# Two gate/up steps on raw x: normalising after the matmul instead of before it

## The chip, the cores and the metric

The kernel runs on one core of one Trainium2 chip. The metric is the device time of one execution in microseconds (us). A core has TensorE (PE in the profile, with its weight loads as PEld), VectorE (DVE), ScalarE (ACT), GpSimd (POOL) and SyncE (SP). SP does no arithmetic here; it issues DMA transfers, and so do ACT and GpSimd. Names such as "SPq" in a profile line mean the issuing queue of that engine.

## The reference, cut to what matters

```python
def reference(A_x, A_w_r, A_w_i, B_x, B_w_gate, B_w_up, B_w_down):
    x = A_x                                        # (1, 2048, 640) bf16
    xn = _layernorm(x, axis=-1)                    # (x - mean) / sqrt(var + 1e-5), per row
    s = irfft2(rfft2(xn) * (w_r + 1j * w_i))       # the spectral branch
    g = _silu((_gelu(xn @ w_gate) * (xn @ w_up)) @ w_down)   # 640 -> 1536 -> 640
    return x + s * g
```

Everything starts from the layer norm of x. The kernel treats the 2,048 rows as 16 slabs of 128 rows and as 4 groups of 512 rows. For each group there are 12 gate/up steps (128 of the 1,536 columns each), and then the down product. The spectral branch is a chain of "folds" (additions on VectorE), Fourier matrices on TensorE, a regrouping through DRAM and the inverse; it fills TensorE between the steps.

## The kernel before

A static planner in the program orders all work on every engine; each piece is added with a rank, an estimated duration and the pieces it comes after. The parts that the change and the argument touch are these.

The start: loads of x and of the first weights, and warm-up matmuls on zeros, which keep TensorE busy until the first slab is ready.

```python
    nc.scalar.dma_start(out=X[64:P, 0, :], in_=xv[64:P, 0, :])
    nc.scalar.dma_start(out=X[:, 2, :], in_=xv[:, 2, :])
    ...
    x_in[0] = dma(X[0:64, 0, :], xv[0:64, 0, :], (0, -4, seq[0]), 163840, use=[sX])
    load_x(1, 2)
    load_x(3, 4)
    ...
    t = keep_warm(8, [t])
    warmed = keep_warm(1, [t, x_in[1]], ns=216)
    load_gu(0, 2)          # Wg and Wu, columns 0 to 255
    load_x(4, 6)
    load_gu(2, 4)
    ...
```

The normalisation of one slab: statistics, the root on GpSimd, the application on VectorE, the transposition on TensorE, and its copy out of PSUM.

```python
            nc.vector.bn_stats(out=STAT[:, n1, 6 * g:6 * g + 6], in_=x[:, 320 * g:320 * g + 320])     # DVE slabs
            nc.scalar.activation(out=junk.tile, in_=x, func=ACT.Square, scale=1.0, bias=NM[:, n1, :], accum_out=var)  # ACT slabs
            ...
            nc.gpsimd.tensor_tensor(out=rstd, in0=var, in1=mh, op=ALU.pow)                            # 1/sigma
            ...
            nc.vector.tensor_scalar(out=sxn.tile[:, n1 % 2, :], in0=X[:, n1, :], scalar1=..., scalar2=RSTD[:, n1, :],
                                    op0=ALU.subtract if eng == "DVE" else ALU.add, op1=ALU.mult)
            ...
                nc.tensor.transpose(out=pt.tile[:, c, :], in_=sxn.tile[:, n1 % 2, c * P:c * P + P], identity=ident)
        turned[n1] = add(lambda e: copy_on(e, xnT[:, :, n1 * P:(n1 + 1) * P], pt.tile), ...)
```

One gate/up step. The first two steps of group 0 are computed slab by slab (128 columns of the result at a time), so that they can begin with the first slab.

```python
            parts = [(128 * j, 128 * j + 128) for j in range(4)] if grp == 0 and t < 2 else [(0, 512)]
            ...
                        nc.tensor.matmul(ps.tile[:, lo:hi], lhsT=w[:, c, t * P:(t + 1) * P],
                                         rhs=xnT[:, c, grp * 512 + lo:grp * 512 + hi], start=(c == 0), stop=(c == 4), ...)
            ...
            nc.scalar.activation(out=ge.tile, in_=pg.tile, func=ACT.Gelu_apprx_tanh)
            nc.vector.tensor_tensor(out=u.tile, in0=pu.tile, in1=ge.tile, op=ALU.mult)
```

Of the kernel before, what the change touches and what calls it, by code (L numbers as in the profile page):

```python
# [11 lines left out]
FP32 = mybir.dt.float32  # L12
# [3 lines left out]
P = 128  # L16
# [98 lines left out]
class Plan:  # L115
# [12 lines left out]
    def add(self, emit, eng, cost, rank, after=(), new=(), use=(), size=0, slow=1.0, hold=0, order=(), lag=0):  # L128
        engs = eng if isinstance(eng, dict) else {eng: cost}
        t = Task(emit=emit, engs=engs, rank=rank, after=list(after), new=list(new), size=size, slow=slow, hold=hold, order=list(order), lag=lag,  # L130
                 seq=len(self.tasks))
        for s in (*new, *use):
            s.users.append(t)
        self.tasks.append(t)
        return t

    def ready(self, t, e, now):
        for a in t.after:
            if a.done is None:
                return None  # L140
        for a in t.order:
            if a.start is None:
                return None
        at = max([0.0] + [a.start + a.engs[e][0] if a.on == e == "PE" else a.done + (0 if a.on == e and not a.size else self.MARGIN[e] + ((2500 if a.size else 250) if e == "PE" and a.start > 20000 else 0)) for a in t.after])
        more = {}
        for s in t.new:
            mine = self.slots[s.tag]
            k = len(mine) - self.bufs[s.tag] + more.get(s.tag, 0)
            more[s.tag] = more.get(s.tag, 0) + 1
            if k >= 0:  # L150
                for u in mine[k].users:
                    if u.done is None:
                        return None
                    at = max(at, u.done + self.MARGIN[e])
        if t.size and e == "SP":
            at = max(at, self.wire - self.BACKLOG)
        return at

    def run(self):
        left, now, order = list(self.tasks), 0.0, []  # L160
        while left:
# [33 lines left out]
            if t.size:  # L195
                self.wire = max(self.wire, now + occ + 900) + t.size * t.slow / 340.0
                t.done = self.wire + (1000 if now < 1000 else 2100 if now < 1700 else 2600 if now < 2700 else 3300 if now < 18000 else 2600 if now < 21000 else 1000) + t.lag
# [22 lines left out]
def kernel(  # L220
# [36 lines left out]
    RSTD = consts.tile([P, NSLAB, 1], FP32)  # L257
    X = persist.tile([P, NSLAB, D], BF16, tag="xb", name="X")
# [5 lines left out]
    D2 = dpool.tile([P, NSLAB, D], BF16)  # L264
    D4 = dpool.tile([NSLAB, 64, 2, LP], BF16)
# [10 lines left out]
    plan = Plan(BUFS, dict(PE=700, DVE=900, ACT=3500, POOL=900, SP=750))  # L276
# [16 lines left out]
    def dma(out, in_, rank, size, after=(), new=(), use=(), slow=1.0, eng=None):  # L293
        return add(lambda e: nc.sync.dma_start(out=out() if callable(out) else out, in_=in_() if callable(in_) else in_),  # L294
                   "SP", (430, 430), rank, after=after, new=new, use=use, size=size, slow=slow)
# [11 lines left out]
    def load_x(a, b):  # L307
        seq[0] += 1
        t = dma(X[:, a:b, :], xv[:, a:b, :], (0, -4, seq[0]), (b - a) * 163840, use=[sX])
        for n in range(a, b):  # L310
            x_in[n] = t
# [8 lines left out]

    def load_gu(a, b):
        cs = slice(a * P, b * P)
        seq[0] += 2
        size = (b - a) * 163840
        i = dma(Wg[:, :, cs], gv[:, :, cs], (0, -4, seq[0] - 1), size, slow=1.1)
        o = dma(Wu[:, :, cs], uv[:, :, cs], (0, -4, seq[0]), size, slow=1.1)
        for t in range(a, b):
            g_in[t], u_in[t] = i, o

    def load_d(h):  # L330
        seq[0] += 1
        t = dma(Wd[:, 6 * h:6 * h + 6, :], dv[:, 6 * h:6 * h + 6, :], (0, -1, seq[0]), 983040)
        for k in range(6 * h, 6 * h + 6):
            d_in[k] = t
# [3 lines left out]
    nc.scalar.dma_start(out=X[64:P, 0, :], in_=xv[64:P, 0, :])  # L338
    nc.scalar.dma_start(out=X[:, 2, :], in_=xv[:, 2, :])
    nc.gpsimd.dma_start(out=ident, in_=tabs["id"])  # L340
    nc.scalar.activation(out=warm, in_=warm, func=ACT.Gelu_apprx_tanh)
# [15 lines left out]
    seq[0] += 1  # L357
    x_in[0] = dma(X[0:64, 0, :], xv[0:64, 0, :], (0, -4, seq[0]), 163840, use=[sX])
    load_x(1, 2)
    load_x(3, 4)  # L360
    x_in[2] = tab_in["id"] = x_in[3]
    t = add(blank, "DVE", (330, 400), (0, -9), new=[idle])
    t = keep_warm(8, [t])
    warmed = keep_warm(1, [t, x_in[1]], ns=216)
    load_gu(0, 2)
    load_x(4, 6)
    load_gu(2, 4)
# [9 lines left out]
    load_d(0)  # L377
    load_d(1)
# [5 lines left out]
    def stats(n1, engs):  # L384
# [19 lines left out]
        if eng == "DVE":  # L404
            t = add(lambda e: half(e, 0), "DVE", (445, 445), (2, n1), after=after, use=[sX])
            t = add(lambda e: half(e, 1), "DVE", (445, 445), (2, n1), after=[t], use=[sX])
            t = add(moments, "DVE", (345, 450), (2, n1, -1), after=[t])
            if n1 == 0:
                keep_warm(2, [warmed, t], ns=216)
        else:  # L410
            t = add(total, "ACT", (940, 1000), (2, n1), after=after, new=[junk], use=[sX])
            t = add(square, "ACT", (1030, 1100), (2, n1), after=[t], use=[junk, sX])
# [7 lines left out]
        if n1 == 0:  # L420
            keep_warm(1, [warmed, t], ns=216)
# [12 lines left out]

    def turn_pe(n1, ap):
        sxn, pt = xn_of[n1 // 2], Slot("sp")

        def mm(e):
            place(pt, (5, P))
            for c in range(5):  # L440
                nc.tensor.transpose(out=pt.tile[:, c, :], in_=sxn.tile[:, n1 % 2, c * P:c * P + P], identity=ident)
        a = add(mm, "PE", c_pe(*[140] * 5), (0, n1), after=[ap, tab_in["id"]], new=[pt], use=[sxn])
        if n1 == 0:
            keep_warm(4, [a], (0, 0, 0), 216)
        turned[n1] = add(lambda e: copy_on(e, xnT[:, :, n1 * P:(n1 + 1) * P], pt.tile),
                         {"DVE": (415, 560)} if n1 == 0 else {"ACT": c_act(640), "DVE": (415, 560)}, None, (0, n1), after=[a], use=[pt], hold=250 if n1 == 0 else 0)
# [61 lines left out]
    lead = ("DVE", "DVE", "ACT", "DVE")  # L508
    for n1 in range(NSLAB):
        if n1 % 2 == 0:  # L510
            xn_of[n1 // 2] = Slot("s1")
        r = stats(n1, (lead[n1] if n1 < 4 else ("ACT" if n1 % 2 else "DVE"),))
        if n1 % 2 == 0:
            aps[n1] = apply(n1, r, True)
        else:
            aps[n1] = apply(n1, r, False)
            aps[n1].after.append(aps[n1 - 1])
        (turn_pe if n1 < 4 else turn_dma)(n1, aps[n1])
        if n1 == 3:
            for j in range(2):  # L520
                fold(j, [aps[k] for k in range(4)])
        elif n1 % 2 and n1 > 3:
            fold(n1 // 2, [aps[n1 - 1], aps[n1]])


# [302 lines left out]
    def gate_up(grp, t):  # L828
# [3 lines left out]
        for w, ps, wt in ((Wg, pg, g_in[t]), (Wu, pu, u_in[t])):  # L832
            parts = [(128 * j, 128 * j + 128) for j in range(4)] if grp == 0 and t < 2 else [(0, 512)]
            mm = []
            for lo, hi in parts:
                def go(e, w=w, ps=ps, lo=lo, hi=hi):
                    if lo == 0:
                        place(ps, (512,))
                    for c in range(5):
                        nc.tensor.matmul(ps.tile[:, lo:hi], lhsT=w[:, c, t * P:(t + 1) * P],  # L840
                                         rhs=xnT[:, c, grp * 512 + lo:grp * 512 + hi], start=(c == 0), stop=(c == 4),
                                         skip_group_check=True)
                step[0] += 1
                rk = (1, step[0]) if len(parts) == 1 else (1, lo // 128 - 10, t)
                mm.append(add(go, "PE", c_pe(*[hi - lo] * 5), rk,
                              after=[wt] + mm[-1:] + [turned[n] for n in range((grp * 512 + lo) // P, (grp * 512 + hi) // P)],
# [3 lines left out]
        def act(e):  # L850
            place(ge, (512,))
            nc.scalar.activation(out=ge.tile, in_=pg.tile, func=ACT.Gelu_apprx_tanh)  # L852

        def mul(e):
            place(u, (512,))
            nc.vector.tensor_tensor(out=u.tile, in0=pu.tile, in1=ge.tile, op=ALU.mult)  # L856
        a = add(act, "ACT", c_act(512), (0, step[0]), after=[last[id(Wg)]], new=[ge], use=[pg], hold=900 if grp == 0 and t < 2 else 0)
        u_done[grp, t] = add(mul, "DVE", c_dve(512, 1, True), (0, step[0]), after=[a, last[id(Wu)]], new=[u], use=[pu, ge])

# [8 lines left out]
    def down(n1):  # L868
# [6 lines left out]
        done = []  # L875
        parts = ((0, 256, "pg"), (256, 512, "pu"), (512, 640, "pg")) if last else ((0, 320, "pg"), (320, 640, "pu"))
# [16 lines left out]
        for lo, hi, tag in parts:  # L893
            ps, th, mm = Slot(tag), Slot("th"), []
            for k in range(0, 12, 6):
                def go(e, k=k, lo=lo, hi=hi, ps=ps):
                    if k == 0:
                        place(ps, (512,))
                    for t in range(k, k + 6):
                        nc.tensor.matmul(ps.tile[:, 0:hi - lo], lhsT=uT[grp, t].tile[:, j * P:(j + 1) * P], rhs=Wd[:, t, lo:hi],  # L900
                                         start=(t == 0), stop=(t == 11))
                step[0] += 1
                mm.append(add(go, "PE", c_pe(*[hi - lo] * 6), (1, step[0]), new=[] if k else [ps],
                              after=[u_done[grp, t] for t in range(k, k + 6)] + mm + [d_in[k]],
                              use=[uT[grp, t] for t in range(k, k + 6)] + ([ps] if k else [])))
# [73 lines left out]
```

## Time and profile before

| | kernel before |
|---|---|
| time, median of 3 runs | 203.61 us (203.57 to 204.02) |
| span of the profiled run | 201.9 us |
| TensorE busy | 195.1 us, 97% |
| granted TensorE clock | 1.0 |
| last matmul ends | 198.03 us |
| first gate matmul | 7.54 us |

These are lines of the profile page of before. The first four cut the span into 40 slices of 5.05 us: busy tenths of TensorE, granted clock in tenths of full speed, busy tenths of the 16 DMA engines, and what they moved. The last is the chain of work that ended last.

```profile
PE   7899999999999999999999999999999999999992
PEclk9999999999999999999999999999999999999999
DMA  5999999899679766524414021069004034443122
GB/s 148 301 324 323 353 379 208 217 210 270 222 255 310 223 145 122 155 57 130 129 45 154 0 68 67 0 176 404 7 0 133 33 98 133 131 130 106 57 68 65
...
PE 93%; DMA 3%; SPq 1%; issue 1%; ACT 0%; DVE 0%; DVEq 0%
```

TensorE is full from the third slice to the last but one and makes up 93% of the chain, so only the two ends hold anything to win. DMA is full as well from 5 to 30 us, at 301 to 379 GB/s. The start, in the timeline of TensorE of before (start, length, engine, line, operation, result and operands, count, and in brackets the idle time ahead of it with what ended it):

```profile
1.21 4.68 PE L354 MATMUL sp<-uT 128*128 128x512 bf16 x12 [1.21 <-DVE uT L347]
6.25 0.45 PE L441 MATMUL sp<-ident,s 128*128 128x128 bf16 x5 [0.36 <-DVE s L430]
6.54 1.03 PE L354 MATMUL sp<-uT 128*128 128x512 bf16 x4
7.54 0.73 PE L840 MATMUL pg<-xnT,Wg 128*128 128x128 bf16 x10
...
15.30 1.24 PE L840 MATMUL pu<-xnT,Wu 128*128 128x512 bf16 x5
```

The first and third lines are warm-ups; the second is the transposition of the first normalised slab, and the fourth the first useful gate matmuls. By about 16.4 us TensorE has finished gate/up steps 0 to 2, four slab transpositions and one fold. Without the fold (0.54 us) that is the mark of 15.84 us: it holds 7.76 us of useful matmuls (16 groups of five 128-column matmuls at 0.28 us, 1.12 us of transpositions and 2.16 us for step 2), so 8.1 us of TensorE time are lost ahead of it.

Two rows of the table by stretches of before (a stretch in us, its length, then the busy share of PE, PEld, DVE, ACT and POOL, the granted clock, the DMA share and GB/s), for comparison later:

```profile
22.00:23.00 1.00, 1.00 (x7) 0.42 (x5) 1.00 (x3) 0.48 (x1) 0.74 (x2) 1.00 1.16 304
24.00:25.00 1.00, 1.00 (x7) 0.48 (x6) 0.97 (x5) 0.87 (x3) 0.00 (x0) 1.00 1.05 381
```

### The profile page before, as it was taken

How to read it: one execution, taken by the hardware profiler on the slowest of the kernel's cores; microseconds unless marked ns; L12 is line 12 of the kernel's file. 1: busy time of each engine (PE TensorE's matmuls, PEld its weight loads, DVE VectorE, ACT ScalarE, POOL GpSimd, SP SyncE). 2: the span in 40 equal slices, each digit the busy share in tenths (PEclk: the TensorE clock that was granted, in tenths of full speed). 3: DMA queues.
4: the chain of work that ended last, by engine and by line, in shares of the span. 5: the costliest groups of instructions: out<-in, count | busy, mean ns of one | idle time of the engine just before them, and what ended most of it. 6: DMA issues, size and time to landing. Idle time of an engine off the chain costs nothing.

```text
span 201.9 us, 3969 instructions
## 1 busy us (share of the span) xinstructions
PE 195.1 (97%) x1467; PEld 115.8 (57%) x1484; DVE 146.6 (73%) x321; ACT 118.5 (59%) x204; POOL 27.1 (13%) x60
## 2 busy tenths in 40 slices
PE   7899999999999999999999999999999999999992
PEld 2584444577545555577765544557764555556771
DVE  3798999992232299999999989522277777776774
ACT  2579888445225777686776654523666676666321
POOL 2478333230000000000000000000001111222100
PEclk9999999999999999999999999999999999999999
DMA  5999999899679766524414021069004034443122
GB/s 148 301 324 323 353 379 208 217 210 270 222 255 310 223 145 122 155 57 130 129 45 154 0 68 67 0 176 404 7 0 133 33 98 133 131 130 106 57 68 65
DMA packets 35284, 32.10 MB, mean 159 GB/s; under 512 B 10806, under 2 KB 32306, under 8 KB 35266
## 3 DMA queue, kind: packets, MB, share of 16 engines
q1 hardware_dynamic: 33714, 28.88, 48.9%
q0 software_dynamic: 1184, 2.70, 5.5%
q10 hardware_dynamic: 368, 0.28, 0.6%
q8 instruction: 11, 0.18, 0.4%
q14 instruction: 7, 0.06, 0.1%
HBM read 22.02 MB, written 9.18 MB: 155 GB/s over the span
## 4 chain that ended last, share of the span: by engine, by line
PE 93%; DMA 3%; SPq 1%; issue 1%; ACT 0%; DVE 0%; DVEq 0%
PE pu L840 25%; PE pg L840 25%; PE pg L900 13%; PE pu L900 13%; DMA Wu<-in_B_w_up_dram 3%; PE sp L653 3%; PE sp L786 3%; PE sp L728 2%; PE sp L762 2%; PE sp L626 2%; PE sp L497 2%; SPq L294 1%; PE sp L646 1%; PE sp L780 1%; PE sp L609 0%
## 5 line engine op out<-in xcount | busy, mean ns | idle before, releaser
L840 PE MATMUL pu<-xnT,Wu 128*128 128x512 bf16 (+1 forms) x264 | 60.2, 355 | 0.6 <-DMA Wu<-in_B_w_up_dram 0.3
L840 PE MATMUL pg<-xnT,Wg 128*128 128x512 bf16 (+1 forms) x259 | 59.1, 354 | 0.7 <-ACT xnT L287 0.2
L856 DVE TENSOR_TENSOR uT<-pu,ge 128x512 bf16<-128x512 f32 x48 | 33.0, 688 | 26.4 <-PE pu L840 23.6
L852 ACT ACTIVATE ge<-pg 128x512 bf16<-128x512 f32 x48 | 28.6, 597 | 34.1 <-PE pg L840 32.1
L900 PEld LDWEIGHTS <-uT 128*128 128x128 bf16 x396 | 37.9, 98 | 13.7
L840 PEld LDWEIGHTS <-Wg 128*128 128x128 bf16 x270 | 24.6, 98 | 24.6 <-DMA Wg<-in_B_w_gate_dram 0.5
L840 PEld LDWEIGHTS <-Wu 128*128 128x128 bf16 x270 | 24.2, 98 | 21.4 <-DMA Wu<-in_B_w_up_dram 0.4
L900 PE MATMUL pg<-Wd,uT 128*128 128x320 bf16 (+2 forms) x204 | 30.5, 293 | 0.0
L900 PE MATMUL pu<-Wd,uT 128*128 128x320 bf16 (+1 forms) x192 | 29.3, 297 | 0.0
L865 POOL DMA_DIRECT2D xr<-in_A_x_dram x16 | 8.7, 544 | 142.3 <-DVE res L888 142.3
L287 ACT CAST ma<-sp 128x644 bf16<-128x644 f32 (+1 forms) x32 | 23.4, 794 | 6.4 <-PE sp L653 4.1
L914 DVE SCALAR_TENSOR_TENSOR G<-th,pg 128x320 bf16<-128x320 f32 (+1 forms) x16 | 7.7, 481 | 9.1 <-ACT th L909 9.0
L909 ACT ACTIVATE th<-pg 128x320 f32<-128x320 f32 (+2 forms) x17 | 7.3, 428 | 11.7 <-PE pg L900 11.4
L914 DVE SCALAR_TENSOR_TENSOR G<-th,pu 128x320 bf16<-128x320 f32 (+1 forms) x16 | 7.7, 482 | 7.8 <-ACT th L909 7.7
L287 ACT CAST mc<-sp 128x640 bf16<-128x640 f32 x16 | 10.6, 692 | 4.3 <-PE sp L498 2.3
L909 ACT ACTIVATE th<-pu 128x320 f32<-128x320 f32 (+1 forms) x16 | 7.0, 438 | 10.2 <-PE pu L900 10.2
L287 ACT CAST Vt<-sp 128x640 bf16<-128x640 f32 x16 | 10.8, 691 | 3.1 <-PE sp L762 3.1
L287 ACT CAST IU<-sp 128x640 bf16<-128x640 f32 x16 | 10.9, 691 | 1.9 <-PE sp L728 1.8
L417 POOL TENSOR_TENSOR RSTD<-MVA,mh 128x1 f32<-128x1 f32 x16 | 9.5, 598 | 13.3 <-DVE MVA L397 12.7
L393 DVE BATCH_NORM_STATS2 STAT<-X 128x6 f32<-128x320 bf16 x18 | 8.7, 485 | 2.8 <-DMA X<-in_A_x_dram 2.8
L287 ACT CAST Z<-sp 128x1024 bf16<-128x1024 f32 x8 | 7.9, 1021 | 1.1 <-PE sp L626 1.1
L706 DVE TENSOR_TENSOR R<-Y 64x644 bf16<-64x644 bf16 x16 | 7.8, 490 | 0.4
(76 smaller groups left out, 209.6 us busy)
## 6 DMA issues: line engine op xcount, KB each, us to landing
BU<-D SPq DMA_DIRECT2D x8, 640.0 KB
D<-mc SPq DMA_DIRECT2D x8, 320.0 KB
xr<-in_A_x_dram POOLq DMA_DIRECT2D x16, 160.0 KB, 3.4
D<-IU SPq DMA_DIRECT2D x8, 320.0 KB
out_dram<-res SPq DMA_DIRECT2D x15, 160.0 KB
Wg<-in_B_w_gate_dram SPq DMA_DIRECT2D x6, 320.0 KB
Wu<-in_B_w_up_dram SPq DMA_DIRECT2D x6, 320.0 KB
Wd<-in_B_w_down_dram SPq DMA_DIRECT2D x2, 960.0 KB
```

Source lines behind the costliest of these rows:

```text
L287: return nc.scalar.copy(out=out, in_=in_) if e == "ACT" else nc.vector.tensor_copy(out=out, in_=in_)
L393: nc.vector.bn_stats(out=STAT[:, n1, 6 * g:6 * g + 6], in_=x[:, 320 * g:320 * g + 320])
L417: nc.gpsimd.tensor_tensor(out=rstd, in0=var, in1=mh, op=ALU.pow)
L653: nc.tensor.matmul(into(q, ri), lhsT=sZ.tile[:, q, ri, :], rhs=FM[:, kinds[q][2] + (4 if ri and kind == 0 else 0), :], start=False, stop=T ...
L706: nc.vector.tensor_tensor(out=o, in0=Yf[:, ::-3, :], in1=Yf[:, 1:3, :], op=ALU.subtract)
L840: nc.tensor.matmul(ps.tile[:, lo:hi], lhsT=w[:, c, t * P:(t + 1) * P], rhs=xnT[:, c, grp * 512 + lo:grp * 512 + hi], start=(c == 0), stop= ...
L852: nc.scalar.activation(out=ge.tile, in_=pg.tile, func=ACT.Gelu_apprx_tanh)
L856: nc.vector.tensor_tensor(out=u.tile, in0=pu.tile, in1=ge.tile, op=ALU.mult)
L865: nc.gpsimd.dma_start(out=sx.tile, in_=xv[:, n1, :])
L900: nc.tensor.matmul(ps.tile[:, 0:hi - lo], lhsT=uT[grp, t].tile[:, j * P:(j + 1) * P], rhs=Wd[:, t, lo:hi], start=(t == 0), stop=(t == 11))
L909: nc.scalar.activation(out=th.tile[:, 0:hi - lo], in_=ps.tile[:, 0:hi - lo], func=ACT.Tanh, scale=0.5)
L914: nc.vector.scalar_tensor_tensor(out=G2.tile[:, lo:hi], in0=th.tile[:, 0:hi - lo], scalar=1.0, in1=ps.tile[:, 0:hi - lo], op0=ALU.add, op1 ...
```

## The change

The idea: (x − mean)/sigma times W equals (x W − mean · colsum(W))/sigma. Steps 0 and 1 of group 0 need therefore not wait for statistics. They multiply x itself, which four DMA transposes bring from DRAM in the layout that TensorE wants (XR). TensorE sums the columns of the weights with 20 one-column matmuls (WSUM). Mean and 1/sigma are needed along the free dimension of the result, while they are computed one per partition; so −mean and 1/sigma of 512 rows are stored to DRAM (D5) and read back as rows broadcast to all partitions (RB). VectorE then applies `(RB1 * WSUM + result) * RB0` to fp32 copies of the four results. Around that: the first loads go to the ACT queue, the statistics of several slabs move from VectorE to ScalarE, step 2 is also computed slab by slab, the down product of group 0 takes steps 0 and 1 last, and margins of the planner are smaller. The change also takes away eight of the sixteen warm-up matmuls of before (8, 1, 2, 1 and 4 of them, at five places ahead of the first gate matmul); only the first eight stay.

```diff
+    for n1 in range(4):
+        raw[n1] = add(lambda e, n1=n1: nc.sync.dma_start_transpose(out=XR[:, :, n1 * P:(n1 + 1) * P], in_=xv[:, n1, :]), "SP", (1400, 1400), (0, -5, n1),
+                      size=1, land=(4300, 5700, 7100, 8500)[n1])
+    for k in ('g', 0, 1, 'u', 2, 3):      # six loads on the ACT queue: Wg, X0, X1, Wu, X2, X3 (cut)
...
+                        nc.tensor.matmul(ps.tile[:, 0, 2 * k + t:2 * k + t + 1], lhsT=w[:, c, t * P:t * P + P], rhs=ones, start=(c == 0), stop=(c == 4),
...
-    lead = ("DVE", "DVE", "ACT", "DVE")
+    lead = ("DVE", "ACT", "DVE", "ACT")
...
+    rs = [dma(D5[k].rearrange("n p -> p n"), t[:, 0:4, 0], (0, -5, 0), 40000, after=[minused] + [roots[n1] for n1 in range(4)], slow=1.0)
+          for k, t in enumerate((RSTD, NM))]
+    rb_in = dma(flat(RB), D5.rearrange("a n p -> (a n p)").partition_broadcast(P), (0, -5, 1), 524288, after=rs)
...
-                                         rhs=xnT[:, c, grp * 512 + lo:grp * 512 + hi], start=(c == 0), stop=(c == 4),
+                                         rhs=XR[:, c, lo:hi] if early else xnT[:, c, grp * 512 + lo:grp * 512 + hi], start=(c == 0), stop=(c == 4),
...
+            m = add(lambda e, ev=ev, k=k: nc.vector.scalar_tensor_tensor(out=ev.tile, in0=RB[:, 1, :], scalar=WSUM[:, 2 * k + t:2 * k + t + 1], in1=ev.tile,
+                                                                         op0=ALU.mult, op1=ALU.add), ...)
+            normed.append(add(lambda e, ev=ev: nc.vector.tensor_tensor(out=ev.tile, in0=ev.tile, in1=RB[:, 0, :], op=ALU.mult), ...))
```

RSTD holds one number per partition and slab, and D5 is laid out as rows. Partition p therefore writes 4 separate elements of 4 bytes. Two such stores make 1,024 elements.

## The prediction

> **What bounds the kernel now.** TensorE. The profile page gives PE 195.1 of 201.9 us busy; the chain of waits is 93% PE; the table of windows shows PE idle at most some 0.1 us in each 20 us from 14 to 198 us, at granted clock 1.0. Only lost PE time at the two ends can be won, and the tail (last matmul ends at 198.0) is not touched. At the start, the PE timeline shows warm-up matmuls until 5.9 us, the first transpose at 6.25, the first gate matmul at 7.54, small gaps to 10 us, none after. By 14.22 us PE has done 16 groups of five 128-column matmuls (0.28 us each, 4.48), four slab transposes (1.12) and the first fold (0.54): 6.14 us of useful work. So 8.1 us are lost, on the sequence x lands (3.7), statistics, root, apply (6.2), transpose, eviction, matmul.
>
> **What the change does.** The first two gate/up steps no longer need statistics: four DMA transposes of x feed them.
> - Removes the wait from x to first matmul. It may start when Wg's first columns and the first transposed slab are in, which I estimate at 4.5 to 5 us (in the trace a load issued at 0.7 us lets DVE start at 3.7; a DMA transpose holds the SP queue 1.23 us).
> - Adds on PE 20 one-column matmuls for column sums: at the 0.056 us of a 128-column matmul about 1.1 us, where PE is the limit.
> - Adds in DMA 0.66 MB of transposes and 0.5 MB of broadcast rows, when DMA is already full (6 to 22 us: share over 1.0, 310 to 330 GB/s). That delays the weights behind by 3 to 4 us. The Trainium skill, "DMA: Bandwidth & Descriptors", section "Issuing engines are not separate DMA queues", says that loads on the ACT queue share the same engines, so moving them there saves issue time only. Step 2 is the tight one: its weights must land by about 12 us; later steps have 3 us or more of slack.
> - Adds on DVE eight fp32 passes of about 0.6 us and some evictions (0.69); about 4 us come back as statistics go to ACT. Windows show DVE at 94 to 96% from 20 to 40 us, so folds and the spectral stage move later by 2 to 3 us. PE has gate and up steps to fill that, and the inverse ends at 185 of 198 us: no cost.
> - Changes the static order everywhere (planning margins): at most the 0.9 us PE idles between 10 and 198 us can be won.
>
> **Sum.** Lost at the start afterwards: 4.75 (start) + 1.1 (column sums) + 0.7 (waiting for Wu and slabs 2, 3: 2.0 MB need some 6.5 us of DMA after 2 us) + 0.4 (step 2 waiting on weights or its eviction) = 6.95, against 8.1. Gain about 1.1 us.
>
> Predicted 202.5 us, range 200.9 to 204.4. Faster by over 2%: 0.04; within 2%: 0.92; slower by over 2%: 0.04.
>
> **What would show it.** The first gate matmul near 4.8 us instead of 7.5; column-sum matmuls of about 1 us in total; PE gaps between 6 and 13 us that end on DMA; normalised steps 0 and 1 finished well before group 0's down stage; PE otherwise full; last fold and regrouping 2 to 3 us later without moving the end.
>
> **What would make it wrong.** Slower: the store of mean and 1/sigma in 4-byte elements (1,024 of them) is slow and the broadcast read behind it blocks the in-order SP queue, so weights come late and PE stands for microseconds; or transposes of DRAM rows are slower than planned. Faster: transposes land early and the sums hide in gaps, for 2.5 us at most.

## The result, and the profile after

| | before | after |
|---|---|---|
| time, median of 4 runs each, same rounds | 203.80 us (203.57 to 204.02) | 215.37 us (214.77 to 216.0) |
| span of the profiled run | 201.9 us | 213.2 us |
| TensorE busy | 195.1 us | 198.7 us |
| mean granted clock | 1.0 | 0.966 |
| first gate matmul | 7.54 us | 6.18 us |
| steps 0 to 2 and four transpositions done | 15.84 us | 19.12 us |

The ratio is 1.0568, with a 95% interval of 1.0532 to 1.0604: the change makes the kernel 5.7% slower. (All ratios in this document are the mean time of one kernel's fast runs over that of the other's of the same rounds, so they are not quite the ratios of the quoted medians.) The prediction of 202.5 us and its range were wrong.

These are lines of the profile page of after that answer to those of before:

```profile
PE   6599927999999999999999999999999999999992
PEclk9769995999999999999999999999999999999999
DMA  6999999996989399675424321011930313333422
GB/s 165 253 326 176 13 209 365 380 251 147 169 246 271 94 350 327 135 125 144 134 67 123 119 70 61 0 65 61 335 160 0 123 52 108 107 111 123 123 95 63
...
PE 82%; DMA 11%; POOL 2%; issue 1%; DVE 1%; ACT 1%; ACTq 0%; DVEq 0%
```

There are two holes in TensorE: one at the start (slices 1 and 2) and a second in slices 6 and 7, from about 27 to 37 us. Each is followed by a stretch at a lower clock. Ahead of the second hole, in slices 4 and 5, the DMA engines count as busy and yet move only 176 and then 13 GB/s, where before moved 323 and 353.

**The first hole.** The timeline of TensorE of after, at the start:

```profile
1.21 3.31 PE L362 MATMUL sp<-uT 128*128 128x512 bf16 x8 [1.21 <-DVE uT L355]
6.18 0.72 PE L881 MATMUL pg<-XR,Wg 128*128 128x128 bf16 x10 [1.66 <-DMA XR<-in_A_x_dram]
6.73 0.39 PE L462 MATMUL sp<-ones,Wg 128*128 128x1 bf16 x10
8.49 1.22 PE L881 MATMUL pg<-XR,Wg 128*128 128x128 bf16 x10 [1.37 <-DMA XR<-in_A_x_dram]
9.51 0.45 PE L462 MATMUL sp<-ones,Wu 128*128 128x1 bf16 x10
9.82 2.29 PE L881 MATMUL pu<-XR,Wu 128*128 128x128 bf16 x20
...
14.75 0.72 PE L881 MATMUL pu<-XR,Wu 128*128 128x128 bf16 x10
```

The first slab of XR lets TensorE start only at 6.18 us, and the second at 8.49. From there on the matmuls run at half speed: ten of them take 1.22 us where the first ten took 0.72 (from start to start 1.02 to 1.07 us against 0.56). The table by stretches gives a granted clock of 0.50 from 8 to 14 us. The Trainium skill, "TensorE: Matmul & The Clock Gate", Part 1, says that the clock halves after an idle window of about 3.4 us and comes back after about as much sustained work. Here two waits of 1.66 and 1.37 us with 0.9 us of short matmuls between them were enough, and the clock stayed low for some 6.5 us. It had only just been raised: the eight warm-ups start 0.40 to 0.43 us after one another, and only the last of them is short (380 ns instead of 634). In before they start 0.22 us after one another by 5.3 us, and more follow until the first gate matmul.

The statistics come late as well, because x itself does. These two lines are from the timeline of ACT of after; the first is the issue of the loads of slabs 2 and 3:

```profile
6.16 0.84 ACTq L369 DMA_DIRECT2D X<-in_A_x_dram x2
7.03 1.28 ACT L385 ACT_TABLE_LOAD   x1 [7.03 <-DMA XR<-in_A_x_dram]
```

The fourth load on the ACT queue was issued by 2.8 us, but the fifth and sixth only at 6.16 us; the trace puts the wait down to a transposed slab. Its records say why: the first eight of these transfers have a semaphore each (a counter by which one engine waits for what another has done), and the fifth load on the ACT queue is given that of the first transpose (number 110) again, so it waits until that transpose has landed. The wait comes from how the program reuses semaphores (e6 below avoids it). VectorE could begin with slab 2 at 10.07 us and ScalarE with slab 3 at 11.75.

**The second hole.** Issues of the SP queue of after (start and length of the issue):

```profile
14.47 0.37 SPq L302 DMA_DIRECT2D D<-RSTD  x1
15.02 0.37 SPq L302 DMA_DIRECT2D D<-NM  x1
...
20.47 6.76 SPq L302 DMA_DIRECT2D X<-in_A_x_dram  x1
28.31 0.37 SPq L302 DMA_DIRECT2D Wg<-in_B_w_gate_dram  x1
29.05 1.79 SPq L302 DMA_DIRECT2D RB<-D  x1
```

The stores leave at 14.47 and 15.02 us. The issue of an x load behind them takes 6.76 us instead of about 0.5, so the next weights (Wg) are issued only at 28.31 and the broadcast read RB at 29.05. The table by stretches of after, with the columns as above:

```profile
18.00:19.00 1.00, 1.00 (x22) 1.00 (x19) 1.00 (x4) 0.97 (x4) 0.56 (x2) 1.00 1.30 194
20.00:21.00 1.00, 1.00 (x8) 0.53 (x7) 1.00 (x4) 1.00 (x4) 0.92 (x3) 1.00 1.15 6
22.00:23.00 1.00, 1.00 (x6) 0.49 (x5) 0.91 (x2) 1.00 (x4) 0.00 (x0) 1.00 0.69 12
24.00:25.00 1.00, 1.00 (x7) 0.49 (x6) 0.00 (x0) 1.00 (x2) 0.00 (x0) 1.00 1.81 10
28.00:29.00 1.00, 0.66 (x4) 0.31 (x5) 0.00 (x0) 0.00 (x0) 0.00 (x0) 1.00 0.45 85
```

For about nine microseconds nearly nothing is moved (6 to 12 GB/s in the three rows between 20 and 25 us; before: 304 and 381 in its two rows). It hits all queues. GpSimd's small copies of the spectral weights, which share only the DMA engines with the stores, took 12.5 to 13.6 us to land instead of 5.3 to 6.2. This agrees with the Trainium skill, "DMA: Bandwidth & Descriptors", section "Issuing engines are not separate DMA queues". GpSimd stands behind its copies (the ninth may start only when the first has landed, as they share a semaphore) and can compute no 1/sigma; VectorE starves (0.00 in the last two rows), and TensorE after it. First the timeline of GpSimd, then that of TensorE, both of after:

```profile
29.05 0.54 POOL L600 DMA_DIRECT2D D<-in_A_w_i_dram  x1 [7.72 <-DMA D<-in_A_w_r_dram]
```

```profile
28.34 1.25 PE L881 MATMUL pg<-xnT,Wg 128*128 128x512 bf16 x5 [1.49 <-DMA Wg<-in_B_w_gate_dram]
32.97 2.29 PE L881 MATMUL pu<-xnT,Wu 128*128 128x512 bf16 x5 [3.38 <-DVE uT L898]
```

TensorE waits 1.49 us for weights and 3.38 us for VectorE, then runs at half clock until 38.3 us, which costs about 2.4 us more (the matmuls from 32.97 us on, from start to start, against 1.08 us for five of 512 columns in before). Together that is 7.3 us. The broadcast read itself is no trouble once it has been issued, and from 40 to 198 us TensorE is as full as before (157.2 of 158 us).

So there were two suspects: the store, for the second hole, and the start on raw x with half the warm-ups, for the first. They had to be separated.

### The profile page after: what moved, and what is told of

Read it like the earlier page. It is cut to its first block, busy times and chain, and to the rows that moved or that the text cites. A ratio compares the mean times of both kernels' runs of the same rounds, so it can differ in the third digit from the quotient of the medians.

```text
span 213.2 us, 4082 instructions
## 1 busy us (share of the span) xinstructions
PE 198.7 (93%) x1508; PEld 120.0 (56%) x1526; DVE 148.1 (69%) x314; ACT 126.5 (59%) x224; POOL 31.7 (15%) x67
## 4 chain that ended last, share of the span: by engine, by line
PE 82%; DMA 11%; POOL 2%; issue 1%; DVE 1%; ACT 1%; ACTq 0%; DVEq 0%
PE pu L881 22%; PE pg L881 20%; PE pg L955 12%; PE pu L955 12%; DMA D<-in_A_w_r_dram 6%; DMA XR<-in_A_x_dram 3%; PE sp L693 3%; PE sp L826 2%; DMA X<-in_A_x_dram 2%; PE sp L768 2%; PE sp L802 2%; PE sp L666 2%; PE sp L528 1%; PE sp L686 1%; PE sp L820 1%
## 5 line engine op out<-in xcount | busy, mean ns | idle before, releaser
L881 PE MATMUL pu<-xnT,Wu 128*128 128x512 bf16 (+1 forms) x237 | 58.1, 371 | 3.9 <-DVE uT L898 3.4
L881 PE MATMUL pg<-xnT,Wg 128*128 128x512 bf16 (+1 forms) x235 | 57.3, 370 | 2.1 <-DMA Wg<-in_B_w_gate_dram 1.5
L894 ACT ACTIVATE ge<-pg 128x512 bf16<-128x512 f32 x46 | 27.5, 597 | 32.9 <-PE pg L881 32.0
L898 DVE TENSOR_TENSOR uT<-pu,ge 128x512 bf16<-128x512 f32 x46 | 31.7, 689 | 21.7 <-PE pu L881 17.6
L881 PEld LDWEIGHTS <-Wg 128*128 128x128 bf16 x285 | 26.5, 103 | 28.3 <-issue 4.8
L881 PEld LDWEIGHTS <-Wu 128*128 128x128 bf16 x285 | 26.5, 104 | 25.9 <-issue 4.2
L964 ACT ACTIVATE th<-pu 128x320 f32<-128x320 f32 (+1 forms) x16 | 7.0, 435 | 11.4 <-PE pu L955 11.1
L437 POOL TENSOR_TENSOR RSTD<-MVA,mh 128x1 f32<-128x1 f32 x16 | 10.7, 670 | 12.7 <-DVE MVA L419 11.8
L425 ACT ACTIVATE th<-X,NM 128x640 bf16<-128x640 bf16 x11 | 9.1, 828 | 0.1
L415 DVE BATCH_NORM_STATS2 STAT<-X 128x6 f32<-128x320 bf16 x10 | 4.6, 486 | 6.5 <-DMA X<-in_A_x_dram 6.5
L422 ACT ACTIVATE th<-X 128x640 bf16<-128x640 bf16 x11 | 8.1, 736 | 1.5 <-DMA X<-in_A_x_dram 1.5
```

Source lines behind the costliest of these rows:

```text
L422: nc.scalar.activation(out=place(junk, (D,)), in_=x, func=ACT.Copy, scale=-1.0 / D, accum_out=NM[:, n1, :])
L894: nc.scalar.activation(out=ge.tile, in_=pg.tile if src is None else src, func=ACT.Gelu_apprx_tanh)
L898: nc.vector.tensor_tensor(out=u.tile, in0=pu.tile if src is None else src, in1=ge.tile, op=ALU.mult)
L964: nc.scalar.activation(out=th.tile[:, 0:hi - lo], in_=ps.tile[:, 0:hi - lo], func=ACT.Tanh, scale=0.5)
```

## The experiments

Fourteen kernels were run, each beside the kernel before on the same chip in the same rounds. The theories are: S, that the stores of 4-byte elements are the cause of the second hole; the rival P, that GpSimd's small copies are; and C, that the halved clock is what the start loses by.

| run | what it is | median us | before in the same rounds | ratio (95%) |
|---|---|---|---|---|
| e1_before_store | before + the two stores, read by nobody | 213.91 | 203.86 | 1.0494 (1.0443 to 1.0544) |
| e2_after_nostore | after, RB read from a constant table | 207.02 | 203.86 | 1.0156 (1.0101 to 1.021) |
| e3_after_16B | after, stored as 16-byte elements | 208.83 | 203.86 | 1.0244 (1.0164 to 1.0324) |
| e4_after_poollate | after, GpSimd's copies late | 214.23 | 203.86 | 1.0509 (1.0458 to 1.056) |
| e5_nostore_warm | e2, more warm-ups | 206.58 | 203.94 | 1.0151 (1.0104 to 1.0198) |
| e6_nostore_order | e2, other order of loads | 208.66 | 203.94 | 1.0216 (1.0184 to 1.0248) |
| e7_nostore_plain | e2, plain loads for the transposes | 207.30 | 203.94 | 1.0166 (1.0132 to 1.02) |
| e8_pebcast | after, rows spread by TensorE, late | 216.42 | 203.94 | 1.0624 (1.0587 to 1.0662) |
| e9_pebcast_warm_order | rows spread early, warm-ups, order | 206.79 | 204.30 | 1.0126 (1.0091 to 1.0161) |
| e10_before_store_rows | as e1, elements 512 bytes apart | 205.72 | 204.30 | 1.0078 (1.0037 to 1.0119) |
| e11_before_load4 | as e1, loads instead of stores | 205.36 | 204.30 | 1.006 (1.0019 to 1.0102) |
| e12_before_store_half | as e1, one store of the two | 210.49 | 204.30 | 1.0311 (1.0257 to 1.0365) |
| e13_repaired_tight | e9, fewer warm-ups | 204.94 | 203.88 | 1.006 (1.0041 to 1.0078) |
| e14_turn_early | e13, transpositions earlier | 204.94 | 203.90 | 1.0043 (1.0017 to 1.007) |

### e1: the store alone, in the kernel before

```diff
+    D5 = dpool.tile([2, 4, P], FP32)
...
+    for k in range(2):
+        dma(D5[k].rearrange("n p -> p n"), RSTD[:, 0:4, 0], (0, -5, 0), 40000, after=[roots[n1] for n1 in range(4)], slow=1.0)
```

> The kernel before with only two stores added (1/sigma of the first four slabs, 2 x 512 elements of 4 bytes, read by nobody), issued behind the loads at about 15 us. Theory S (the 4-byte store clogs the DMA engines): within a few us of its issue DMA throughput falls from 320 GB/s to under 50 for some 10 us at full DMA share, PE stands for some us, time 207 to 213 us. Rival P (the 12 small GpSimd loads that the change moved to 15 us are what clogs): they stay at 10 us here, so no collapse, and time within 1 us of 203.8.

Measured: 213.91 us against 203.86, so 10.1 us for 4 KB that nobody reads. The table by stretches, and the wait of TensorE in its timeline, of this run:

```profile
18.00:19.00 1.00, 1.00 (x7) 0.49 (x6) 0.97 (x5) 1.00 (x3) 0.47 (x1) 1.00 0.04 13
22.00:23.00 1.00, 1.00 (x6) 0.47 (x5) 0.00 (x0) 0.42 (x2) 0.53 (x2) 1.00 0.84 29
```

```profile
35.13 0.59 PE L498 MATMUL sp<-mb,F1T 128*128 128x512 bf16 x1 [4.87 <-DVE s L431]
```

It is the same picture as in after: throughput falls to 13 to 88 GB/s for nine microseconds, and TensorE later stands 4.87 us (and 1.57 and 0.71 us elsewhere), followed by half clock. There is no transpose and no broadcast read in this kernel, so neither is needed for the second hole. The store is sufficient. Nor has the planner shuffled anything: on TensorE, VectorE, ScalarE and GpSimd the trace of e1 shows the same order of work as that of before.

### e2: the change without the store

```diff
-    rs = [dma(D5[k].rearrange("n p -> p n"), t[:, 0:4, 0], ...) for k, t in enumerate((RSTD, NM))]
-    rb_in = dma(flat(RB), D5.rearrange("a n p -> (a n p)").partition_broadcast(P), (0, -5, 1), 524288, after=rs)
+    const = nc.inline_tensor(np.concatenate([np.full(512, 20.0), np.zeros(512)]).astype(np.float32), name="tab_rb").ap()
+    rb_in = dma(flat(RB), const.partition_broadcast(P), (0, -5, 1), 524288, after=[minused] + [roots[n1] for n1 in range(4)])
```

The constants stand in for 1/sigma and −mean, so steps 0 and 1 are only approximately right. The comparison with the reference does not notice it, since s·g is small beside x; so in this kernel and those made from it (e5 to e7) it says nothing about correctness.

> The kernel after, with the broadcast rows read from a constant table, so that the store falls away and everything else stays (result only approximate, on purpose). S: no collapse of DMA throughput between 18 and 29 us, no PE stall at 27 to 37 us and no second stretch of half clock; what is left is the slow start: 206 to 208.5 us. P: the small GpSimd loads still start at 15 us and still take 13 us; time stays over 212.

Measured: 207.02 us. The 512 KB broadcast read is still there and the collapse is gone (307 to 365 GB/s from 18 to 26 us). A row of its table by stretches:

```profile
22.00:23.00 1.00, 1.00 (x7) 0.53 (x6) 1.00 (x3) 1.00 (x3) 0.98 (x3) 1.00 1.18 307
```

So of the 11.6 us that after loses, 8.4 (215.37 − 207.02) go with the store and 3.2 (207.02 − 203.86) remain. The timeline of TensorE of this run:

```profile
1.21 3.59 PE L362 MATMUL sp<-uT 128*128 128x512 bf16 x8 [1.21 <-DVE uT L355]
6.43 1.22 PE L881 MATMUL pg<-XR,Wg 128*128 128x128 bf16 x10 [1.62 <-DMA XR<-in_A_x_dram]
...
8.71 1.23 PE L881 MATMUL pg<-XR,Wg 128*128 128x128 bf16 x10 [0.81 <-DMA XR<-in_A_x_dram]
...
10.04 2.29 PE L881 MATMUL pu<-XR,Wu 128*128 128x128 bf16 x20
...
18.57 0.44 PE L881 MATMUL pu<-xnT,Wu 128*128 128x128 bf16 x5
```

Steps 0 to 2 and the four transpositions are done at 18.85 us, 3.0 us behind the 15.84 of before. That is nearly the whole rest of 3.2 us, and after 20 us TensorE stays full. Ten matmuls take 1.22 us here from the very first, though the page records a clock of 1.00 in this run; the durations decide. (The skill's page on the clock gate warns, under "HAM trace caveats", that such records can be unreliable.) All eight warm-ups were slow as well (the eighth took 634 ns), so here the clock had never been raised. The traces of all seven kernels with eight warm-ups sort this way: where the eighth was short (after, e3, e7), the first ten matmuls run at full clock; where it was not (e2, e4, e6, e8), at half. With 12 or more warm-ups (before, e5, e9, e13, e14) they run at full clock.

### e3: the same data in 16-byte elements

```diff
-    D5 = dpool.tile([2, 4, P], FP32)
+    D5 = dpool.tile([2, P, 4], FP32)
...
-    rs = [dma(D5[k].rearrange("n p -> p n"), t[:, 0:4, 0], ...)
+    rs = [dma(D5[k], t[:, 0:4, 0], ...)
```

VectorE then reads RB with a stride. The result is right.

> The kernel after, right result, with the store as 2 x 128 elements of 16 bytes (the four slabs of a partition together) and VectorE reading the rows strided. S by number of elements: a quarter of the collapse, about 2.5 us, mostly hidden; 206.5 to 209 us. If the collapse came from a store to DRAM as such, or from the read behind it, it stays and so does the time, over 212. P: over 212.

Measured: 208.83 us; RB is issued at 21.60 us instead of 29.05. There are 256 elements of 16 bytes in place of 1,024 of 4 bytes, in the same 4 KB of DRAM. The lowest row of the table by stretches between 16 and 24 us has 229 GB/s, so a dip is left but no collapse. The run is 1.8 us slower than e2; part of that is a wait of 1.0 us of the down product for corrected steps 0 and 1. It is no way back to the time of before.

### e4: GpSimd's small copies moved behind the last 1/sigma

```diff
-  ... "POOL", (600, 600), (9, ri, b, a), after=[roots[3]], size=5152))
+  ... "POOL", (600, 600), (9, ri, b, a), after=[roots[15]], size=5152))
```

> The kernel after, with the 12 small GpSimd loads moved behind the last 1/sigma (about 40 us). P: the collapse is gone and the time falls to 206 to 209 us. S: DMA throughput still falls under 50 GB/s for about 10 us after the store, weights and x still come late, PE still stalls; VectorE no longer waits 7 us for GpSimd, which gives back 0 to 2 us: 213 to 216.

Measured: 214.23 us, with the collapse still there (20, 5, 2, 12 GB/s from 19 to 23 us). The rival P falls: those copies are victims. That GpSimd stands behind them is worth about 1 us (215.37 − 214.23).

### e10, e11, e12: what it is about the store

```diff
 e10 -    D5 = dpool.tile([2, 4, P], FP32)
     +    D5 = dpool.tile([2, 4, P, 128], FP32)
     +        dma(D5[k, :, :, 0].rearrange("n p -> p n"), RSTD[:, 0:4, 0], ...)
 e11 +    c4 = nc.inline_tensor(np.ones((2, 4, P), np.float32), name="tab_c4").ap()
     +        dma(LD[:, k, :], c4[k].rearrange("n p -> p n"), ...)
 e12 -    for k in range(2):
     +    for k in range(1):
```

All three start from e1. In e10 the same 1,024 elements of 4 bytes go out, but each lands in a DRAM row of its own of 512 bytes. In e11 1,024 elements of 4 bytes are loaded from 4 KB of DRAM instead. In e12 only one of the two stores is made.

> As e1_before_store, same 1,024 elements of 4 bytes, but each to its own 512-byte row of DRAM. If elements next to each other collide (several engines rewriting the same line), the collapse goes and the time is 204 to 206 us. If every small DRAM write costs by itself, DMA throughput falls just as in e1_before_store and the time is 212 to 215.

> As e1_before_store, but 1,024 loads of 4 bytes from DRAM into SBUF instead of stores. If the number of descriptors is what costs, the same collapse and 212 to 215 us; if it is the write to DRAM, no collapse and 203.8 to 205.

> As e1_before_store with one of the two stores, 512 elements. By number of elements: DMA throughput under 100 GB/s for about 5 us instead of 9 to 10, and less than half of the 10 us of loss, as the weights have some slack: 205 to 209 us.

Measured over before in the same rounds: 1.4 us for e10, 1.1 us for e11, 6.2 us for e12, where e1 had 10.1. The expectation for e12 missed: half of the elements should have cost less than half of 10.1 us, and at 6.2 they did not. Rows of the table by stretches of e10, at the same places as those of e1:

```profile
18.00:19.00 1.00, 1.00 (x6) 0.49 (x5) 0.70 (x4) 1.00 (x3) 1.00 (x3) 1.00 0.59 111
22.00:23.00 1.00, 1.00 (x7) 0.41 (x6) 1.00 (x3) 0.68 (x2) 0.91 (x2) 1.00 1.13 433
```

So neither the number of elements nor their size is by itself the main cost: the same 1,024 writes 512 bytes apart disturb DMA for about four microseconds, and 1,024 loads of 4 neighbouring bytes for about two. Even the 1.4 and 1.1 us need not be the price of these elements: the two extra transfers hold the SP queue for some 2 us, and the next x load is issued at 14.61 us in e10 and 15.09 in e11 instead of 12.85. What costs 10 us is that many small writes go next to each other in DRAM. How many and how small still counts there: e3 has 256 elements of 16 bytes in the same 4 KB, and only a dip. The Trainium skill, "DMA: Bandwidth & Descriptors", "Specifications", says that below 512 bytes a transfer becomes a read-modify-write. That holds for e10 as well and is cheap there, so the page's sentence alone does not explain e1. That neighbouring read-modify-writes have to wait for each other would fit, but is not shown: e10 changed the distance and, with it, the size of the region (512 KB instead of 4).

### e5: full clock at the start

```diff
-            for k in range(n):
+            for k in range(2 * n):                       # 16 warm-up matmuls instead of 8
...
+                    for i in range(6) if early and lo == k == 0 and t == 1 else (): nc.tensor.matmul(heat.tile[...], ...)   # 6 more between slabs
```

This starts from e2.

> The kernel after without its store (constant rows, as in e2_after_nostore) and with more warm-up matmuls: 8 more before the first transposed slab and 6 more between the first and the second, program order else the same. Theory C (the gaps at the start let the TensorE clock fall to half, and that costs as much as the gaps): the early matmuls then run 0.56 us per ten instead of 1.07, PE reaches the slab transposes at about 13 us instead of 15, and the time falls from 207.0 to 205 to 206 (the fourth slab's x, which lands late, then holds it). Rival D (the start is bound by DMA alone, the clock is harmless): within 0.4 us of 207.0.

Measured: 206.58 us, against 207.02 for e2 in another round; the ratios, 1.0151 and 1.0156, are the same. The timeline of TensorE of this run:

```profile
6.77 0.72 PE L881 MATMUL pg<-XR,Wg 128*128 128x128 bf16 x10
...
13.03 0.72 PE L474 MATMUL sp<-ident,s 128*128 128x128 bf16 x10
15.71 0.69 PE L474 MATMUL sp<-ident,s 128*128 128x128 bf16 x5 [1.95 <-DVE xnT L295]
```

The clock works as C says: ten early matmuls take 0.72 us, and the transpositions begin at 13.03 us instead of 15.04. But the 2 us are not kept. TensorE now waits 1.95 us for the slab chain, because slab 3 of x has landed late (its statistics start at 12.02 us, and the copy that TensorE waits for stands in VectorE's queue behind the application to slab 3, at 14.81). In the profiled run, the slowest of the four (208.51; the others had 206.3 to 206.7), the clock fell again there. C was right that the clock costs the time, and wrong about the gain: behind the clock stood the arrival of x. Whether the gaps or the missing warm-ups take the clock away is not separated, as the run mends both.

### e6: the loads of x earlier

```diff
-    for k in ('g', 0, 1, 'u', 2, 3):
+    for k in ('g', 'u', 0, 2):                           # Wg, Wu, X[0:2], X[2:4]: four loads instead of six
```

This too starts from e2.

> As e2_after_nostore, with ACT's six loads as four: Wg, Wu, then x in two loads of two slabs, so that all eight first transfers go out without waiting for the semaphore of a transpose. Theory L (in the kernel after, ACT's loads of x slabs 2 and 3 stand until 6.2 us behind the first transposed slab, and so their statistics are late): slabs 2 and 3 land near 9 us instead of 10 and 11.7; alone worth 0 to 1 us while the clock is still halved: 206 to 207. If nothing waits there: 207.0 and unchanged landing.

Measured: 208.66 us (207.65 to 209.64), above e2's 207.02 (the intervals of the two ratios overlap a little), a miss. At the start it does what it should: slabs 2 and 3 land at about 8.8 us instead of 10 to 12, the second slab is multiplied at 7.57 us without a gap, and steps 0 to 2 are done at 17.42 us. But the time is lost again in the profiled run (the slowest of the four) at 70 us, in this line of its timeline:

```profile
70.52 1.07 PE L666 MATMUL sp<-T,BU 128*128 128x128 bf16 x16 [2.09 <-DMA BU<-D]
```

The spectral stage reaches its regrouped data before they have come back from DRAM. The half clock that follows, in two groups of five 512-column matmuls, costs about 1.7 us more. The regrouping reads were issued at 55.26 us in before and at 66.19 here. The corrections of steps 0 and 1 on VectorE can be only part of that: e13 below has them too and issues these reads at 59.32 us. The rest is not explained. In e2 the same lateness (64.72 us) was free, because TensorE came later too.

### e7: plain loads in place of the transposes

```diff
-        nc.sync.dma_start_transpose(out=XR[:, :, n1 * P:(n1 + 1) * P], in_=xv[:, n1, :])
+        nc.sync.dma_start(out=XR[:, :, n1 * P:(n1 + 1) * P], in_=xv[:, n1, :].rearrange("p (c k) -> p c k", c=5))
```

The layout of XR, and so the product, is wrong; the work and the bytes are the same. It starts from e2.

> As e2_after_nostore, with the four DMA transposes replaced by plain loads of the same bytes into the same tile (wrong result on purpose). If transposing itself makes the slabs late, the first gate matmul starts at 4.7 to 5.2 us instead of 6.4 and the second slab follows without the 0.8 to 1.4 us gap; time 203.5 to 205.5. If it is only the number of bytes in front, the first gate matmul stays at 6 us or later and the time at 206.5 to 207.

Measured: 207.30 us, no gain on e2. The first gate matmul starts at 5.08 us instead of 6.43, so transposing in DMA costs at least 1.35 us of the start (e7 then waits for Wg, not for x); in the second slice of the page DMA moves 291 GB/s here and 232 in e2. (The Trainium skill, "DMA: Bandwidth & Descriptors", "Latency and other measured facts", gives a lower effective bandwidth, 261 GB/s, for one kind of transpose; the trace agrees in direction, with other loads mixed in.) But then Wu lands only at 9.33 us, TensorE stands 1.87 us for it, and after the wait it runs at half clock until about 14.5 us, which costs 1.6 us more (start to start). That the sum of bytes binds, since x comes twice, is the likely reading; the run does not separate it from the clock.

### e8: the rows spread by TensorE, a miss of mine

```diff
+            for n in range(4):
+                nc.tensor.matmul(pr.tile[:, a, n * P:n * P + P], lhsT=ST[:, a, n:n + 1].to_broadcast([P, P]), rhs=ident, start=True, stop=True, ...)
+    t = add(spread, "PE", c_pe(*[128] * 8), (1, 45), after=[minused], new=[pr])
+    rb_in = add(lambda e: copy_on(e, flat(RB), flat(pr.tile)), ...)
```

Store and broadcast read are gone. Eight matmuls multiply a column of 1/sigma or −mean, repeated along the free dimension, by the identity; the product is the row in all partitions.

> The kernel after, right result, with the rows of -mean and 1/sigma spread over the partitions by eight 128-column matmuls against the identity (bf16) instead of over DRAM: neither the store nor the 0.5 MB read. Expected 206.3 to 207.5 us: like e2_after_nostore, plus 0.5 us of PE, less the 0.5 MB of DMA.

Measured: 216.42 us. There is no collapse of DMA. But I had given the spreading too late a rank: it ran at 43.53 us, the corrections from 45 to 52 us, and the down product of group 0 had to wait for them. The timeline of TensorE:

```profile
49.16 0.31 PE L964 MATMUL pg<-Wd,uT 128*128 128x320 bf16 x1 [3.66 <-DVE uT L907]
52.43 0.45 PE L964 MATMUL pg<-Wd,uT 128*128 128x320 bf16 x1 [2.96 <-DVE uT L907]
```

The half clock that followed added to it. The run says nothing against spreading on TensorE; it shows that about 7 us of VectorE work on steps 0 and 1 has a deadline.

### e9, e13, e14: the repaired idea

e9 is e8 with the spreading early (rank 26.5), the order of e6, and the warm-ups of e5. e13 is e9 with 12 warm-ups in all ahead of the first slab and none between the slabs. e14 is e13 with the transpositions of slabs 0 and 1 among the last early matmuls. All three give right results.

```diff
 e9  -    t = add(spread, "PE", c_pe(*[128] * 8), (1, 45), after=[minused], new=[pr])
     +    t = add(spread, "PE", c_pe(*[128] * 8), (1, 26.5), after=[minused], new=[pr])
 e13 -            for k in range(2 * n):
     +            for k in range(n + 4):
 e14 -        a = add(mm, "PE", c_pe(*[140] * 5), (0, 6, n1), after=[ap], new=[pt], use=[sxn])
     +        a = add(mm, "PE", c_pe(*[140] * 5), (0, 5, 300 - n1 % 2, -1) if n1 < 2 else (0, 6, n1), after=[ap], new=[pt], use=[sxn])
```

> The change with all three repairs together, right result: rows spread by matmuls (now early, right behind the third step, so that the corrections of steps 0 and 1 are not late as in e8_pebcast), more warm-up matmuls, and four loads on ACT instead of six. If the start is the sum of the named losses (clock, slab 3, store), the third step ends at about 16 us, within 0.5 us of the kernel before at the same work, and the time is 203.5 to 205.5 us. If the later folds (regrouping 10 us later than before) cost PE time as in e6_nostore_order, 206 to 208.

> As e9_pebcast_warm_order (206.8 us, 2.5 us over the kernel before), but with 12 warm-up matmuls instead of 16 in front and none of the 6 between the slabs, since with the new order of loads the second slab lands right behind the first. If the rest of e9's loss is that surplus of warm-up (first gate matmul at 7.4 instead of 6.3, and 1.3 us between the slabs), PE reaches the slab transposes at 11.5 to 12.5 us instead of 13.7 and the time is 204.3 to 205.8. If the fourth slab's statistics bind instead, PE waits longer before the third transpose and the time stays at 206 to 207. Under 203 (better than before) only if both go well.

> As e13_repaired_tight (204.9 us), but the transposes of normalised slabs 0 and 1 stand among the last early matmuls, so that their evictions do not queue behind ACT's evictions of steps 0 and 1; e13 showed a PE gap of 0.85 us there. If that gap is worth its length, 204.0 to 204.4 us, level with the kernel before (203.9). If the normalised slabs are ready later than placed, PE waits there instead and nothing is won: 204.7 to 206. Under 203.4, clearly better than before, is not expected, as column sums and row spreading still cost PE about 1 us.

Measured: 206.79 us for e9, where 16 warm-ups held the first gate matmul back to 7.40 us; 204.94 us for e13 and for e14, where before had 203.88 and 203.90. The timeline of TensorE of e13:

```profile
6.31 0.72 PE L890 MATMUL pg<-XR,Wg 128*128 128x128 bf16 x10 [0.97 <-DMA XR<-in_A_x_dram]
...
11.55 0.72 PE L473 MATMUL sp<-ident,s 128*128 128x128 bf16 x10
13.12 0.72 PE L473 MATMUL sp<-ident,s 128*128 128x128 bf16 x10 [0.85 <-ACT xnT L294]
```

Both holes are gone: full clock from the first gate matmul on, no collapse, no later wait of TensorE. What is left is a kernel 0.4 to 0.6% slower than before. Steps 0 to 2 and the transpositions are done at 16.46 us in e13 (without half a fold that runs ahead), 0.6 us behind before, and the last matmul ends at 198.66 us instead of 198.03. The start won 1.2 us (6.31 against 7.54), but 0.77 us went to the column sums and the gaps around them, 0.45 to spreading the rows, and 1.0 to the wait for slabs 2 and 3, where before had small gaps only. In e14 that wait changed its place and the time stayed. About 0.4 us more of the profiled span lies in the tail and is not explained. No version that was tried beats before.

## Why the prediction was wrong

**The failed step, 8.4 of 11.6 us: the store.** The prediction's sum has no term for it. It stands only under "What would make it wrong": "the store of mean and 1/sigma in 4-byte elements (1,024 of them) is slow and the broadcast read behind it blocks the in-order SP queue". The suspect was right, but it was given a chance of 0.04, and its way was only half seen. It is not the broadcast read that blocks (e2 has that read and no hole, e1 has no such read and the hole). The stores take down the throughput of all DMA for nine microseconds, on other queues as well. e1 puts the price at 10.1 us in the kernel before, and e2 at 8.4 in after. The bytes, 4 KB, told nothing; nor did the count of 1,024 elements, which costs at most 1.4 us where they lie 512 bytes apart (e10).

**The second failed step, 3.2 us: "Lost at the start afterwards: 4.75 (start) + 1.1 (column sums) + 0.7 (waiting for Wu and slabs 2, 3 …) + 0.4 (step 2 …) = 6.95, against 8.1".** Against the mark of steps 0 to 2 done, with 7.76 us of useful matmuls ahead of it (the prediction's own mark was one stage earlier; the loss of before is 8.1 us at both):

| us lost | predicted | e2 | after |
|---|---|---|---|
| until the first gate matmul | 4.75 | 6.43 | 6.18 |
| column sums | 1.1 | 0.76 | 0.70 |
| waits for slabs of XR or for Wu | 0.7 | 0.81 | 1.37 |
| half clock | not in the sum | 2.6 | 2.6 |
| wait and gap at the transpositions, before step 2 | 0.4 | 0.5 | 0.5 |
| sum | 6.95 | 11.1 | 11.4 |

(The half clock is worked out from start-to-start times over 0.56 us for ten 128-column matmuls.) The largest term is the one that was missing: the change drops eight of the sixteen warm-ups and starts earlier with gaps, and so loses the clock that before had reached and kept. The second is the landing of the transposed slab, 1.4 to 1.7 us later than estimated. "Slabs 2 and 3" were in the sum, yet as bytes only; that their loads would be issued at 6.16 us was not seen. As e5 shows, these terms hide each other: repairing the clock alone gained nothing, because the late slabs were waiting behind it.

**Right: TensorE bounds the kernel and only the ends can be won.** In e2 the 3.2 us are those of the start, within 0.2.

**Right: the column sums are cheap.** About 0.25 us for ten at full clock in e13, and 0.7 us for all in after, where 1.1 was predicted.

**Right in kind: DMA is full and delays what stands behind.** TensorE's early gaps did end on DMA, and in e7 TensorE waits for Wu even without the transposing.

**Partly wrong: "folds and the spectral stage move later by 2 to 3 us", at no cost.** The regrouping reads were issued 9.5 us later in e2 (64.72 against 55.26) and 4.1 us later in e13 (59.32). The passes of VectorE took 0.75 and 0.69 us instead of 0.6. It cost nothing in e2, where TensorE was late as well, but a wait of 2.1 us in e6. "No cost" held by luck.

**Right: the smaller margins of the planner gave next to nothing.** From 40 to 198 us TensorE is busy 157.3 us in before and 157.2 in after.

**What stays open.** Why small writes next to each other hold up all of DMA is not shown, only that for 1,024 elements of 4 bytes their nearness decides. Whether the dropped warm-ups or the gaps cost more of the clock at the start was not tested apart, nor why the folds come as late as they do in e6. In e13 and e14 the last 1 us is divided by reading the trace, not by an experiment for each part.

## What to carry to other kernels

Before moving data through DRAM to turn a column into a row, ask how many elements of a few bytes land next to each other: 4 KB stored that way cost 10 us here, while eight small matmuls against the identity did the same work in 0.45 us of TensorE. An earlier start is worth only what stays gapless after it: keep enough warm-up work ahead of the first matmul (eight left the clock low or barely raised here, twelve did not), and check that the second and third pieces of data come as early as the first. When several waits stand behind each other at a start, count lost time to a mark behind all of them, since repairing one shows only the next.

## What the Trainium skill lacked or had wrong

- "DMA: Bandwidth & Descriptors" has the read-modify-write below 512 bytes, but not that many such writes side by side in DRAM stop nearly all DMA: 1,024 elements of 4 bytes in 4 KB cost 10.1 us, with 13 to 88 GB/s for nine microseconds (e1); 512 of them cost 6.2 us (e12); 1,024 of them 512 bytes apart cost 1.4 us (e10); and 1,024 loads cost 1.1 us (e11); the last two include the 2 us for which the extra transfers hold their queue.
- The same page, "Rules for kernel authors", says to coalesce small transfers because they are mostly overhead. That rule names no cost for other queues, and no passage of the page puts one on small stores to DRAM: GpSimd's copies took 12.5 to 13.6 us to land instead of 5.3 to 6.2.
- "TensorE: Matmul & The Clock Gate", Part 1, gives a length, about 3.4 us, only for one whole idle window; for shorter gaps it gives none. Two waits of 1.66 and 1.37 us with 0.9 us of short matmuls between them gave half clock for some 6.5 us in after, where the clock had been raised no more than about 0.5 us before the first of them.
